# Retention attention fused with a two-layer MLP: attention work of two tiles grouped on TensorE, and PSUM laid out as named double banks

## Chip, cores, metric

One core of one Trainium2 chip. The metric is device time in microseconds of one execution; most executions of one kernel agree within 0.3%. In the profile PE is TensorE (matmuls), PEld its weight loads, DVE VectorE, ACT ScalarE, POOL GpSimd and SP the engine that issues most DMAs. The span is the time from the first to the last instruction of the profiled run.

## The reference

```python
# q, k, v: (8, 8, 576, 64); w_in: (512, 2048); w_out: (2048, 512); all f32
scores = (q @ k.transpose(0, 1, 3, 2)) / 8
gamma  = 1 - 2.0 ** (-5 - arange(8))                  # one per head
D      = where(i >= j, gamma ** (i - j), 0)           # causal decay
x      = ((scores * D) @ v).transpose(0, 2, 1, 3).reshape(4608, 512)
h      = x @ w_in
out    = (h * cos(h)) @ w_out
```

## The kernel before

The tokens are cut into 36 tiles of 128. For each tile: `prep` scales q and k by powers of gamma, `transposes` turns them, `scores` makes the products within the tile (64-row matmuls, two heads at a time in the array), which DVE then masks into `ret`, `state` carries the sum over earlier tiles of a sequence, `attn_out` adds both parts (full matmuls for the state, then matmuls of 64 columns for the tile itself) and casts the result to `xT`. Blocks of 512 tokens (two of 256 near the start) then go through `mm1` (h, cosine, product) and `mm2` (o). The attention of the next block is put between the o matmuls of the present one. Both kernels divide PSUM, where matmul results go, into eight banks of 512 f32 columns; an h tile is what one cosine and one product then read.

```python
widths = [512, 256, 256] + [512] * 7
ps_sc = tc.tile_pool(name="ps_sc", bufs=1, space=PSUM)    # scores: 2 banks
ps_st = tc.tile_pool(name="ps_st", bufs=1, space=PSUM)    # state: 1
ps_ov = tc.tile_pool(name="ps_ov", bufs=1, space=PSUM)    # attention output: 1
ps_mm = tc.tile_pool(name="ps_mm", bufs=4, space=PSUM)    # h, o, transposes: 4
# ... cut
def attn_out(g):
    ps = ps_ov.tile([P, HG, P], F32, tag="ov")
    if c > 0:                              # 4 matmuls 128x128 with the state
        # ... cut
    for hg in range(HG):                   # 8 matmuls of 64 columns
        for he in range(2):
            nc.tensor.matmul(ps[he*D : he*D+D, hg, :], lhsT=vb[:, 2*hg+he, :],
                             rhs=ret[:, he, hg, :], ...)
    nc.vector.tensor_copy(xT[:, :, g*P : (g+1)*P], ps)

def units(g0, g1):                         # order of the attention pieces
    # transposes (early tiles), scores(g), attn_out(g - 1), state(g), ...
    # ... cut
def mm1(n, et, c0, w):
    ps = ps_mm.tile([P, 512 // w, w], F32, tag="mm", name="h")
    # matmuls into one bank, then
    nc.scalar.activation(cosh, ps, ACTF.Sin, bias=half_pi, scale=1.0)
    nc.vector.tensor_mul(gT[:, et : et + m, c0 : c0 + w], ps, cosh)
# ... cut: in each block the units are spread evenly between the 64 mm2 calls
```

## Time and profile before

| | before |
|---|---|
| median of 16 runs | 326.04 us (325.43 to 327.14) |
| span of the profiled run | 324.5 us |
| PE / DVE / ACT / POOL busy | 94% / 59% / 41% / 30% |
| first h matmul of block 1, 2, 3, 4 and 9 (PE timeline) | 58.48, 76.06, 96.24, 129.30, 293.19 us |
| one middle block of 512 tokens | 32.51 or 33.06 us |

Blocks are counted from 0; 1 and 2 are the small ones. The stretch up to the first h matmul of block 1 is set by arriving data, the rest by PE. Blocks 4 to 7 have these two lengths in turn because the work repeats every nine tiles (two sequences of 576 tokens), and the first and the last of the nine skip four state matmuls each: a block that holds both has 217 matmuls, the others 225. Line numbers (L272 and so on) are those of each kernel by itself. The lines that the argument rests on are in the prediction.

### The profile page before, as it was taken

Reading aid. Unit: us, or ns where it says so; the run is one execution under the profiler, and the core shown is the slowest. Engines: PE = TensorE matmul, PEld = TensorE weight load, DVE = VectorE, ACT = ScalarE, POOL = GpSimd, SP = SyncE. Lnnn points to the kernel's source line nnn. Section 1 sums busy time; section 2 is a strip of 40 time slices with the busy share of each in tenths; the row PEclk is TensorE's granted clock in tenths of the full one; section 3 lists DMA queues with packets and bytes.
Section 4 is the critical chain, followed back from the end, with each engine's and each line's share of the span. In section 5 each row is a group of like instructions: output and inputs, shape, how many; then the busy total and the mean of one; then the engine's idle time right before and its main releaser. Section 6 shows DMA issues by size and latency. Waiting matters only on the chain.

```text
span 324.5 us, 5550 instructions
## 1 busy us (share of the span) xinstructions
PE 306.6 (94%) x2176; PEld 160.9 (50%) x2176; DVE 192.1 (59%) x267; ACT 133.8 (41%) x204; POOL 97.8 (30%) x120
## 2 busy tenths in 40 slices
PE   2687999999899999999999999999999999999995
PEld 1565844857554445444444454444445444454442
DVE  2765705565877854685468646864686558645800
ACT  4344722544218511751176107610761067016711
POOL 3370057644463635430543054305430000000000
PEclk9999999999999999999999999999999999999999
DMA  9999999999999999935993599449942500010011
GB/s 171 216 124 209 210 205 244 225 211 217 187 237 199 258 214 254 225 68 134 207 253 58 134 237 211 67 113 252 215 71 65 129 35 3 32 68 32 0 67 65
DMA packets 151514, 49.65 MB, mean 153 GB/s; under 512 B 142784, under 2 KB 146368, under 8 KB 151488
## 3 DMA queue, kind: packets, MB, share of 16 engines
q1 hardware_dynamic: 147264, 45.10, 72.7%
q0 software_dynamic: 4224, 4.19, 8.1%
q8 instruction: 17, 0.28, 0.4%
q14 instruction: 9, 0.07, 0.1%
HBM read 36.70 MB, written 9.44 MB: 142 GB/s over the span
## 4 chain that ended last, share of the span: by engine, by line
PE 83%; DMA 8%; SPq 5%; POOL 2%; issue 1%; ACT 0%; DVE 0%; DVEq 0%
PE o L272 38%; PE h L256 34%; DMA w_out_sb<-in_moe_w_out_dram 5%; SPq L102 5%; PE ov L219 3%; PE sc L155 3%; DMA fq<-in_q_dram 3%; PE st L183 2%; PE ov L209 2%; POOL w_in_sb L334 1%; POOL qks L125 1%; PE tr L142 0%; DVE ret L164 0%; POOL qks L126 0%; ACT cosh L264 0%
## 5 line engine op out<-in xcount | busy, mean ns | idle before, releaser
L272 PE MATMUL o<-w_out_sb,gT 128*128 128x512 bf16 x576 | 142.5, 380 | 0.4 <-DMA w_out_sb<-in_moe_w_out_dram 0.4
L256 PE MATMUL h<-xT,w_in_sb 128*128 128x512 bf16 (+1 forms) x704 | 127.7, 342 | 2.3 <-DMA w_in_sb<-in_moe_w_in_dram 2.3
L265 DVE TENSOR_TENSOR gT<-h,cosh 128x512 bf16<-128x512 f32 x144 | 99.5, 691 | 47.8 <-ACT cosh L264 47.8
L264 ACT ACTIVATE cosh<-h,half_pi 128x512 f32<-128x512 f32 x144 | 98.9, 687 | 31.3 <-PE h L256 31.3
L256 PEld LDWEIGHTS <-w_in_sb 128*128 128x128 bf16 x704 | 69.0, 98 | 59.5 <-DMA w_in_sb<-in_moe_w_in_dram 2.8
L281 ACT COPY ot<-o 128x512 f32<-128x512 f32 x36 | 21.1, 585 | 143.6 <-PE o L272 143.6
L125 POOL TENSOR_TENSOR qks<-fq,gq 128x512 bf16<-128x512 f32 x36 | 37.5, 1042 | 127.8 <-DMA fq<-in_q_dram 116.1
L272 PEld LDWEIGHTS <-gT 128*128 128x128 bf16 x576 | 49.6, 98 | 52.0 <-issue 0.7
L164 DVE TENSOR_TENSOR ret<-sc,tri 128x1024 bf16<-128x1024 f32 x32 | 39.1, 1222 | 20.6 <-PE sc L155 20.5
L227 DVE CAST xT<-ov 128x512 bf16<-128x512 f32 x36 | 24.8, 689 | 19.1 <-PE ov L219 19.0
L126 POOL TENSOR_TENSOR qks<-fk,gk 128x512 bf16<-128x512 f32 x32 | 33.3, 1042 | 3.9 <-DMA fk<-in_k_dram 2.5
L192 DVE TENSOR_TENSOR sb<-st,diag 128x512 bf16<-128x512 f32 x32 | 22.0, 688 | 13.2 <-PE st L183 13.1
L132 POOL CAST vb<-fv 128x512 bf16<-128x512 f32 x32 | 19.5, 610 | 9.0 <-DMA fv<-in_v_dram 7.3
L155 PE MATMUL sc<-qkT 64*128 64x128 bf16 x288 | 15.2, 228 | 4.2 <-ACT qkT L147 2.9
L155 PEld LDWEIGHTS <-qkT 64*128 64x128 bf16 x288 | 8.7, 98 | 18.8 <-issue 13.2
L219 PE MATMUL ov<-ret,vb 128*64 128x128 bf16 x288 | 15.8, 234 | 1.6 <-DVE ret L164 1.6
L147 ACT COPY qkT<-tr 128x512 bf16<-128x512 bf16 x16 | 8.8, 589 | 12.0 <-PE tr L142 12.0
L183 PEld LDWEIGHTS <-qks 128*128 128x128 bf16 (+1 forms) x128 | 9.6, 101 | 8.1 <-issue 2.5
L209 PEld LDWEIGHTS <-sb 128*128 128x128 bf16 x128 | 10.1, 102 | 7.0
L183 PE MATMUL st<-vb,qks 128*128 128x128 bf16 (+1 forms) x128 | 13.3, 230 | 0.0
L219 PEld LDWEIGHTS <-vb 128*64 128x64 bf16 x288 | 10.0, 114 | 6.2 <-issue 3.4
L209 PE MATMUL ov<-qkT,sb 128*128 128x128 bf16 (+1 forms) x128 | 12.7, 224 | 0.0
(29 smaller groups left out, 35.2 us busy)
## 6 DMA issues: line engine op xcount, KB each, us to landing
out_dram<-ot SPq DMA_DIRECT2D x36, 256.0 KB, 3.7
fq<-in_q_dram SPq DMA_DIRECT2D x32, 256.0 KB, 4.2
fk<-in_k_dram SPq DMA_DIRECT2D x32, 256.0 KB, 4.6
fv<-in_v_dram SPq DMA_DIRECT2D x32, 256.0 KB, 4.9
w_out_sb<-in_moe_w_out_dram POOLq DMA_DIRECT2D x4, 512.0 KB, 17.9
w_in_sb<-in_moe_w_in_dram POOLq DMA_DIRECT2D x1, 1024.0 KB, 12.7
fq<-in_q_dram SPq DMA_DIRECT2D x8, 128.0 KB, 4.0
fk<-in_k_dram SPq DMA_DIRECT2D x8, 128.0 KB, 4.1
```

Source lines behind the costliest of these rows:

```text
L125: nc.gpsimd.tensor_tensor(out=qks[:, 0], in0=fq, in1=tq, op=ALU.mult)
L126: (nc.vector if early else nc.gpsimd).tensor_tensor(out=qks[:, 1], in0=fk, in1=tk, op=ALU.mult)
L155: nc.tensor.matmul(ps[:, he, hg, :], lhsT=qkT[d0 : d0 + D, HG + hg, :], rhs=qkT[d0 : d0 + D, hg, :], start=True, stop=True,)
L164: nc.vector.tensor_tensor(out=ret.rearrange("p a b i -> p (a b) i"), in0=ps.rearrange("p a b i -> p (a b) i"), in1=mask.unsqueeze(1).to_br ...
L183: nc.tensor.matmul(ps[:, hg, :], lhsT=qks[p0:, 1, 2 * hg : 2 * hg + 2, :].rearrange("s h d -> s (h d)"), rhs=vb[p0:, 2 * hg : 2 * hg + 2, ...
L209: nc.tensor.matmul(ps[:, hg, :n], lhsT=sb[:, hg, :], rhs=qkT[:, hg, :n], start=(hg == 0), stop=False, skip_group_check=True,)
L219: nc.tensor.matmul(ps[he * D : he * D + D, hg, :], lhsT=vb[:, 2 * hg + he, :], rhs=ret[:, he, hg, :], start=(c == 0 and hg == 0), stop=(hg ...
L227: nc.vector.tensor_copy(xT[:, :, g * P : (g + 1) * P], ps)
L256: nc.tensor.matmul(ps[:, j, :], lhsT=w_in_sb[:, dg, (et + j) * P : (et + j + 1) * P], rhs=xT[:, dg, t0 : t0 + w], start=(dg == 0), stop=(d ...
L264: nc.scalar.activation(cosh, ps, ACTF.Sin, bias=half_pi, scale=1.0)
L265: nc.vector.tensor_mul(gT[:, et : et + m, c0 : c0 + w], ps, cosh)
L272: nc.tensor.matmul(ps, lhsT=gT[:, et, tsi * P : (tsi + 1) * P], rhs=w_out_sb[:, et, :], start=(et == 0), stop=(et == ET - 1),)
```

## The change

Its intent: let the attention pieces of two neighbouring tiles run together, and let ACT and DVE work on 1024 columns at a time. For that the PSUM pools become named buffers in one pool: a, b and m of two banks each, n and st of one. Besides, w_in is loaded in four equal pieces, two small products move from DVE to POOL, and block 3 runs in half widths so that it can start before its second half is ready. Not shown in the cut below: x is kept in one rotating tile for each block, some SBUF pools have a buffer more, the o tiles that share a double bank are called `oo`, and the places of the attention pieces are now fixed numbers.

```diff
-    ps_sc/ps_st/ps_ov (bufs=1), ps_mm (bufs=4)
+    psum = ctx.enter_context(tc.tile_pool(name="psum", bufs=1, space=bass.MemoryType.PSUM))
@@ prep
-        (nc.vector if early else nc.gpsimd).tensor_tensor(
+        (nc.vector if early and g in (0, 3) else nc.gpsimd).tensor_tensor(
@@ attn_out, now for a list of tiles
+        ps = psum.tile([P, len(gs), HG, P], F32, tag=bank, name="ov")
+        for x, g in enumerate(gs):      # all full matmuls with the state first
...
+        for x, g in enumerate(gs):      # then all matmuls of 64 columns
...
+        nc.vector.tensor_copy(tiles["x", n][...], ps)      # one cast for the pair
@@ mm1
-        m = 512 // w
+        m = 1024 // w
-        ps = ps_mm.tile([P, m, w], F32, tag="mm", name="h")
+        ps = psum.tile([P, m, w], F32, tag=bank, name="h")
@@ loads
-            load_w_in(0, 256); load_w_in(256, 512); load_w_in(512, 1024); load_w_in(1024, 2048)
+            for e in range(0, DF, 512):
+                load_w_in(e, e + 512)
@@ placement between the o matmuls
+    def pair(g, banks, sc, av):
+        mid = (sc + av) // 2
+        return [
+            (sc - 5, lambda: state(g)),
+            (sc, lambda: (scores(g, banks[0]), scores(g + 1, banks[1]))),
+            (mid, lambda: state(g + 1)),
+            (av, lambda: attn_out([g, g + 1], banks[0])),
+        ]
...
+        banks = {0: "bambambam", 1: "bmab", 2: "bmab", 3: "mamabmab"}.get(n, "bmabmabm")
...
+        elif n == 2:
+            todo = pair(g, "ab", 11, 24) + pair(g + 2, "ba", 31, 40)[:2]
+            late += [lambda: (state(g + 3), attn_out([g + 2, g + 3], "b"))]   # inside block 3
+        elif n + 1 < len(widths):
+            todo = pair(g, "ab", 12, 26) + pair(g + 2, "ab", 41, 56)
```

More of the change, by code (lines that the diff above doesn't have):

```diff
@@ L60 @@
     trp = ctx.enter_context(tc.tile_pool(name="trp", bufs=8))
-    retp = ctx.enter_context(tc.tile_pool(name="retp", bufs=3))
-    stp = ctx.enter_context(tc.tile_pool(name="stp", bufs=3))
+    retp = ctx.enter_context(tc.tile_pool(name="retp", bufs=4))
+    stp = ctx.enter_context(tc.tile_pool(name="stp", bufs=4))
     gp = ctx.enter_context(tc.tile_pool(name="gp", bufs=2))
@@ L65 @@
     op = ctx.enter_context(tc.tile_pool(name="op", bufs=4))
-    ps_sc = ctx.enter_context(tc.tile_pool(name="ps_sc", bufs=1, space=bass.MemoryType.PSUM))
-    ps_st = ctx.enter_context(tc.tile_pool(name="ps_st", bufs=1, space=bass.MemoryType.PSUM))
-    ps_ov = ctx.enter_context(tc.tile_pool(name="ps_ov", bufs=1, space=bass.MemoryType.PSUM))
-    ps_mm = ctx.enter_context(tc.tile_pool(name="ps_mm", bufs=4, space=bass.MemoryType.PSUM))
+    xp = ctx.enter_context(tc.tile_pool(name="xp", bufs=3))
+    psum = ctx.enter_context(tc.tile_pool(name="psum", bufs=1, space=bass.MemoryType.PSUM))
     ctx.enter_context(tc.manual_schedule())
@@ L86 @@
     w_out_sb = consts.tile([P, ET, DM], BF16)
-    xT = consts.tile([P, DG, NTOK], BF16)
     tiles = {}
@@ L132, in prep, with transposes @@
             nc.gpsimd.tensor_copy(vb, tiles.pop(("fv", g)))
-    def transposes(g):
+    def transposes(g, early=False):
         qks, vb, qkT = tiles["a", g]
@@ L139, in transposes @@
         for m in range(2):
-            ps = ps_mm.tile([P, HG, P], BF16, tag="mm", name="tr")
+            ps = psum.tile([P, 2 * HG, P], BF16, tag=("bn" if early else "ba" if g < 6 else "ma")[m], name="tr")
             for hg in range(HG):
@@ L146, in transposes, with scores @@
                 )
-            nc.scalar.copy(qkT[:, m * HG : (m + 1) * HG, :], ps)
-    def scores(g):
+            nc.scalar.copy(qkT[:, m * HG : (m + 1) * HG, :], ps[:, :HG, :])
+    def scores(g, bank):
         qks, vb, qkT = tiles["a", g]
-        ps = ps_sc.tile([P, 2, HG, P], F32, tag="sc", name="sc")
+        ps = psum.tile([P, 2, HG, P], F32, tag=bank, name="sc")
         for hg in range(HG):
@@ L178, in state @@
         if first:
-            tiles["stps"] = ps_st.tile([P, HG, P], F32, tag="st", name="st")
+            tiles["stps"] = psum.tile([P, HG, P], F32, tag="st", name="st")
         ps = tiles["stps"]
@@ L198, in state, with attn_out @@
         tiles["sb", g + 1] = sb
-    def attn_out(g):
-        c = g % PER
-        qks, vb, qkT = tiles.pop(("a", g))
-        ret = tiles.pop(("ret", g))
-        ps = ps_ov.tile([P, HG, P], F32, tag="ov", name="ov")
-        if c > 0:
+    def attn_out(gs, bank):
+        ps = psum.tile([P, len(gs), HG, P], F32, tag=bank, name="ov")
+        for x, g in enumerate(gs):
+            c = g % PER
+            if c == 0:
+                continue
+            qkT = tiles["a", g][2]
             sb = tiles.pop(("sb", g))
@@ L209, in attn_out @@
                 nc.tensor.matmul(
-                    ps[:, hg, :n],
+                    ps[:, x, hg, :n],
                     lhsT=sb[:, hg, :],
@@ L216, in attn_out @@
                 )
-        for hg in range(HG):
-            for he in range(2):
-                nc.tensor.matmul(
-                    ps[he * D : he * D + D, hg, :],
-                    lhsT=vb[:, 2 * hg + he, :],
-                    rhs=ret[:, he, hg, :],
-                    start=(c == 0 and hg == 0),
-                    stop=(hg == HG - 1),
-                    skip_group_check=True,
-                )
-        nc.vector.tensor_copy(xT[:, :, g * P : (g + 1) * P], ps)
-    def units(g0, g1):
-        u = []
-        if g0 < min(g1, N_PE_T):
-            u.append(lambda g=g0: transposes(g))
-        for g in range(g0, g1):
-            if g + 1 < min(g1, N_PE_T):
-                u.append(lambda g=g + 1: transposes(g))
-            u.append(lambda g=g: scores(g))
-            if g > g0:
-                u.append(lambda g=g - 1: attn_out(g))
-            if g % PER < PER - 1:
-                u.append(lambda g=g: state(g))
-        if g1 > g0:
-            u.append(lambda g=g1 - 1: attn_out(g))
-        return u
@@ L246, in mm1 @@
-    def mm1(n, et, c0, w):
+        for x, g in enumerate(gs):
+            vb = tiles.pop(("a", g))[1]
+            ret = tiles.pop(("ret", g))
+            for hg in range(HG):
+                for he in range(2):
+                    nc.tensor.matmul(
+                        ps[he * D : he * D + D, x, hg, :],
+                        lhsT=vb[:, 2 * hg + he, :],
+                        rhs=ret[:, he, hg, :],
+                        start=(g % PER == 0 and hg == 0),
+                        stop=(hg == HG - 1),
+                        skip_group_check=True,
+                    )
@@ L248, in mm1 @@
+        n = max(m for m in range(len(starts)) if starts[m] <= gs[0] * P)
+        if ("x", n) not in tiles:
+            tiles["x", n] = xp.tile([P, DG, 512], BF16, tag="xT", name="xT")
+        t0 = gs[0] * P - starts[n]
+        nc.vector.tensor_copy(
+            tiles["x", n][:, :, t0 : t0 + len(gs) * P].rearrange("p c (x i) -> p x c i", i=P), ps
+        )
+    def mm1(n, et, c0, w, bank):
         if ("g", n) not in tiles:
             tiles["g", n] = gp.tile([P, ET, 512], BF16, tag="gT", name="gT")
-        gT = tiles["g", n]
@@ L251, in mm1 @@
-        m = 512 // w
-        t0 = starts[n] + c0
-        ps = ps_mm.tile([P, m, w], F32, tag="mm", name="h")
+        gT, xT = tiles["g", n], tiles["x", n]
+        m = 1024 // w
+        ps = psum.tile([P, m, w], F32, tag=bank, name="h")
         for j in range(m):
@@ L258, in mm1 @@
                     lhsT=w_in_sb[:, dg, (et + j) * P : (et + j + 1) * P],
-                    rhs=xT[:, dg, t0 : t0 + w],
+                    rhs=xT[:, dg, c0 : c0 + w],
                     start=(dg == 0),
@@ L268, in mm2 @@
         gT = tiles["g", n]
+        wide = tsi == 0 if n == 2 else tsi in (1, 3)
         if et == 0:
-            tiles["o", n, tsi] = ps_mm.tile([P, DM], F32, tag="mm", name="o")
-        ps = tiles["o", n, tsi]
+            if not wide:
+                tiles["o"] = psum.tile([P, DM], F32, tag="n", name="o")
+            elif tsi < 2:
+                tiles["oo"] = psum.tile([P, 2, DM], F32, tag="m", name="oo")
+        ps = tiles["oo"][:, tsi // 2, :] if wide else tiles["o"]
         nc.tensor.matmul(
@@ L347 @@
         if g == 3:
-            load_w_in(0, 256)
-            load_w_in(256, 512)
-            load_w_in(512, 1024)
-            load_w_in(1024, 2048)
+            for e in range(0, DF, 512):
+                load_w_in(e, e + 512)
             w_dma = [load_w_out(e, e + 4) for e in range(0, ET, 4)]
@@ L356 @@
             nc.gpsimd.memset(tri_mix[:HP, HP:], 0.0)
-        transposes(g)
+        transposes(g, early=True)
         nc.scalar.copy(tiles["a", g][1], tiles.pop(("fv", g)))
-        scores(g)
+        scores(g, "a")
         if g < 3:
@@ L363 @@
         if g < 3:
-            attn_out(g)
+            attn_out([g], "m")
     for g in (4, 5):
@@ L367 @@
     loaded = prepared = transposed = 6
-    first = [(0, 0), (0, 4), (1, 0), (0, 8), (1, 4), (0, 12), (1, 8), (1, 12)]
-    for i, (half, et) in enumerate(first):
-        mm1(0, et, half * 256, 256)
-        if i == 0:
-            attn_out(3)
-        mm1(0, et + 2, half * 256, 256)
-    for n, w in enumerate(widths):
-        if n > 0:
-            for et in range(0, ET, 512 // w):
-                mm1(n, et, 0, w)
-        todo = []
-        if n + 1 < len(widths):
-            g0 = starts[n + 1] // P
-            todo = units(g0, g0 + widths[n + 1] // P)
-        nts = w // P
-        mms = [(tsi, et) for tsi in range(nts) for et in range(ET)]
-        lo, hi = (len(mms) // 2, len(mms) - 4) if n == 0 else (2, len(mms) - 6)
-        place = [lo + (hi - lo) * i // max(1, len(todo) - 1) for i in range(len(todo))]
+    def pair(g, banks, sc, av):
[6 more added lines that the diff above has]
+        ]
@@ new lines, in pe_transposes @@
+    def pe_transposes(g, place):
+        return [(place, lambda: transposes(g)), (place + 6, lambda: transposes(g + 1))]
+    late = []
+    for n, w in enumerate(widths):
+        if n in (0, 3):
+            halves = [(0, 0), (0, 4), (1, 0), (0, 8), (1, 4), (0, 12), (1, 8), (1, 12)]
+            if n == 3:
+                halves.sort()
+            blocks = [(et, half * 256, 256) for half, et in halves]
+        else:
+            blocks = [(et, 0, w) for et in range(0, ET, 1024 // w)]
+        banks = {0: "bambambam", 1: "bmab", 2: "bmab", 3: "mamabmab"}.get(n, "bmabmabm")
+        for i, (et, c0, cw) in enumerate(blocks):
+            mm1(n, et, c0, cw, banks[i])
+            if n == 0 and i == 0:
+                attn_out([3], "m")
+            if n == 3 and i == 1:
+                late.pop()()
+        g = starts[n] // P + w // P
+        if n == 0:
+            todo = [(28, lambda: transposes(g)), (40, lambda: transposes(g + 1))]
+            todo += pair(g, "ab", 46, 58)
+        elif n == 1:
+            todo = pe_transposes(g, 1) + pair(g, "ab", 13, 26)
+        elif n == 2:
[3 more added lines that the diff above has]
+            todo = pair(g, "ab", 12, 26) + pair(g + 2, "ab", 41, 56)
+        else:
+            todo = []
+        todo.sort(key=lambda u: u[0])
+        mms = [(tsi, et) for tsi in range(w // P) for et in range(ET)]
@@ L389 @@
         for i, (tsi, et) in enumerate(mms):
-            while place and place[0] <= i:
-                place.pop(0)
-                todo.pop(0)()
+            while todo and todo[0][0] <= i:
+                todo.pop(0)[1]()
             mm2(n, tsi, et)
+        assert not todo
 _INS = ['q', 'k', 'v', 'moe_w_in', 'moe_w_out']
```

## The prediction

> **What bounds the kernel now.** I read the page first, then the chain that ended last, then the TensorE timeline around single insertions. The page, and the chain by engine:
>
> ```profile
> span 324.5 us, 5550 instructions
> PE 306.6 (94%) x2176; PEld 160.9 (50%) x2176; DVE 192.1 (59%) x267; ACT 133.8 (41%) x204; POOL 97.8 (30%) x120
> ...
> DMA  9999999999999999935993599449942500010011
> ...
> PE 83%; DMA 8%; SPq 5%; POOL 2%; issue 1%; ACT 0%; DVE 0%; DVEq 0%
> ```
>
> PE is the bound: it makes 83% of the chain, and the rest (DMA, SP's queue, POOL) lies in the first 50 us, where operands are still arriving. DVE at 59% and ACT at 41% have room. But 94% busy does not mean 94% of what PE can do, so I looked at steady blocks of 512 tokens (64 matmuls of h, 64 of o, and the attention of four 128-token tiles put between the o matmuls). Windows from block start to block start; the columns are length, then busy time of PE, PEld, DVE, ACT, POOL, then clock, DMA share and GB/s:
>
> ```profile
> 129.47:161.98 32.51, 32.51 (x217) 15.36 (x216) 20.61 (x27) 13.33 (x20) 10.55 (x13) 1.00 0.84 161
> 161.98:195.04 33.06, 33.06 (x225) 15.77 (x224) 21.29 (x28) 13.33 (x20) 11.33 (x13) 1.00 0.88 169
> ```
>
> PE never idles here, so only the start-to-start distance of its matmuls can shrink. In the chain the 64 h matmuls of a block take 13.81 us, 0.216 each. Around a scores insertion (8 matmuls with 64 rows), a state insertion (4 matmuls of 128x128) and an output insertion (4 full matmuls, then 8 with 64 columns), the PE timeline reads (start, length, what):
>
> ```profile
> 143.33 0.38 PE L272 MATMUL o<-w_out_sb,gT 128*128 128x512 bf16 x1
> 143.64 0.40 PE L155 MATMUL sc<-qkT 64*128 64x128 bf16 x8
> 143.97 0.39 PE L272 MATMUL o<-w_out_sb,gT 128*128 128x512 bf16 x1
> ```
>
> ```profile
> 145.06 0.39 PE L183 MATMUL st<-vb,qks 128*128 128x128 bf16 x4
> 145.28 0.38 PE L272 MATMUL o<-w_out_sb,gT 128*128 128x512 bf16 x1
> ```
>
> ```profile
> 148.09 0.39 PE L209 MATMUL ov<-qkT,sb 128*128 128x128 bf16 x4
> 148.41 0.41 PE L219 MATMUL ov<-ret,vb 128*64 128x128 bf16 x8
> 148.76 0.39 PE L272 MATMUL o<-w_out_sb,gT 128*128 128x512 bf16 x1
> ```
>
> State: 145.06 to 145.28 is 0.22 for four, 0.055 each, nothing lost. Scores: o starts at 143.33 and the scores at 143.64, 0.31 where 0.216 is normal, so 0.095 lost on entry; scores to o is 0.33 where eight matmuls running in twos need 4 x 0.055 = 0.22, so 0.11 lost on exit. Output: 148.09 to 148.41 is 0.32 for four full matmuls that need 0.22 (0.10 lost), and 148.41 to 148.76 is 0.35 for 0.22 (0.12 lost, rounded up). **Every visit to a 64-row or 64-column shape costs 0.21 to 0.22 us**, and a block of four tiles makes eight such visits: 1.7 us in 33.
>
> What PE waits for, other than that (engine, line, whom; us in total, times, longest), from the waits of PE:
>
> ```profile
> PE h L256 <- DMA w_in_sb<-in_moe_w_in_dram: 2.3, 2, 1.3
> PE ov L219 <- DVE ret L164: 1.6, 3, 0.9
> PE sc L155 <- DVE ret L164: 1.3, 1, 1.3
> ...
> PE o L272 <- DMA w_out_sb<-in_moe_w_out_dram: 0.4, 1, 0.4
> PE tr L142 <- POOL qks L126: 0.4, 1, 0.4
> ```
>
> Only the third lies after 60 us (at 85.8 us): the single scores buffer is still being read.
>
> **What the Trainium skill says.** "TensorEngine Tiling (Array Packing)", Key Properties: changing the tiling mode drains the TensorE, changing only the tile does not. The trace agrees: 0.095 to 0.12 us at each change between full and 64-wide shapes, none between o and st. "TensorE: Matmul & The Clock Gate", Back-to-back issue gap, gives N/2.4 + 2.5 ns: 216 ns at 512 columns and 56 at 128; the trace has 0.216 and 0.055. "Trainium Kernel Development and Optimization", Performance Expectations, warns that matmul busy time is a poor metric since matmuls are pipelined; here one o matmul is listed at 380 ns while the next starts after 216. "PSUM — Partial Sum Buffer", PSUM bank collisions, asks for guarding by bank: a bank that DVE or ACT is reading is closed to PE. That decides whether fewer, wider buffers can rotate; the 1.3 us wait above is such a case.
>
> **The change part by part.**
> 1. *Pairing.* Scores of two tiles run back to back, then later the outputs of two tiles (all full matmuls first, then all sixteen of 64 columns). Four visits per pair become two: 2 x 0.215 = 0.43 us saved. Tiles 4 to 35 are paired, 16 pairs: 16 x 0.43 = **6.9 us**, all on PE's path. Tiles 0 to 3 stay single.
> 2. *The wait at 85.8 us* goes, since two scores buffers exist: **-1.3**. In its place the block of tokens 1024 to 1535 starts with its second h tile in the bank of a scores read just issued: about 1.7 us of h matmuls against two reads of 1.22 us each (the `ret` row of the page's groups) plus a start-up: my estimate **+0.3**.
> 3. *h in two banks* (1024 columns): 72 cosines and 72 products instead of 144 each. DVE takes 0.691 us for 512 columns and 1.22 for 1024 (`ret`), so 99.5 us of products become about 72 x 1.22 = 88; ACT saves some too. Neither is on the path: **0**. What can hurt is the latency: after PE ends a 1.73 us tile, cosine (at most 1.22) and product (1.22) hold its banks for 2.5 us, but with three double banks PE returns after 2 x 1.73 = 3.46. The first o matmul that needs the last product is the 15th, 14 x 0.216 = 3.0 us later. Both hold with 0.5 to 1 us to spare.
> 4. *Block 3 in half widths*: 128 x 0.109 (6.99 us for 64 in the chain) against 64 x 0.216: **+0.15**.
> 5. *Start.* Before 43 us DMA sets the pace. The first two w_in transfers, 256 columns each, become one of 512, and packets double. While they ran, the DMA view gives the first line below, later the second:
>
> ```profile
> DMA packets 1107, 0.59 MB, mean 132 GB/s; under 512 B 32, under 2 KB 1106, under 8 KB 1106
> ...
> DMA packets 1703, 2.07 MB, mean 207 GB/s; under 512 B 48, under 2 KB 1332, under 8 KB 1703
> ```
>
> 0.59 MB at 207 would take 2.9 us instead of 4.5; I credit about half, 0.8. PE's own waits on w_in (2.3 us) vanish or shrink, but they are worth nothing by themselves: the o matmuls then start earlier and wait for the last w_out piece, which landed at 43.04 and only moves by what the DMA stream gains. After that, later transposes (index 28 and 40 instead of 32 and 35) avoid the 0.4 us wait for POOL. Together **-1.2**. The products for k of tiles 1 and 2 move from DVE (0.68) to POOL (1.04), which otherwise idles for q: hidden, **0**.
> 6. *Casts of 1024 columns* (0.69 becomes about 1.22) six o matmuls (1.3 us) ahead of the next block in the two small blocks, and transposes there into a bank just used: **+0.2**.
>
> Sum: -6.9 - 1.3 + 0.3 + 0.15 - 1.2 + 0.2 = -8.75, so 325.9 becomes 317.1; I say 317.0. The tail (last o, copy, store) stays.
>
> **Rivals.** (a) *PSUM becomes the new wait.* Eight banks are now shared by named buffers used one at a time, and one late reader stops PE in every block. For: the margins in 3 are under 1 us and DVE runs its queue in order. Against: DVE is 59% busy and will be less. A stall of 0.5 us in each of seven blocks would give 320.5; 1 us would give 324. (b) *The drain is not saved by adjacency*: the loss belongs to each scores group and not to the change of shape, or two groups in different banks drain too. For: the view before shows no two groups of one shape in a row. Against: inside a group, eight matmuls take 0.22 plus exactly one exit. Then only items 2, 4, 5 and 6 remain, -1.85: 324.0. (c) *The start gains nothing*, as DMA is full from 18 to 150 us and q/k/v behind it come no sooner: 318.3. (d) *The start gains more*, with the whole w_in and w_out stream over a microsecond sooner: 316.
>
> **Range and chances.** The pairing term is counted from the trace and I trust it within 1 us; the stalls can only add, up to about 3 us, and the start can give 1 us more. So 314.5 to 320.5. The 2% line is at 319.4: faster 0.80, same 0.19, slower 0.01.
>
> **What would show each step.** Blocks from the fourth on should be 0.85 us shorter (32.2 and 31.65 instead of 33.06 and 32.51). Scores should come as 16 in about 0.66 us from entry to exit, with one entry loss of 0.095 and one exit of 0.11. The waits of PE should show no more than a few tenths on cosines, products, `ret` or casts; if they show over 2 us there, rival (a) holds and I am too low. If paired groups are as long as two single ones, (b) holds. The last w_out wait should end near 42.2 us rather than 43.04. The PE total of busy time should fall to about 298 us, and the h products on DVE should be 72 of about 1.22 us.

## The result

The changed kernel takes **317.31 us** (median of 8 runs, 316.98 to 317.88) against 326.04. The ratio is 0.9733, with a 95% interval of 0.9722 to 0.9743. The forecast was 317.0.

The page after: PE still makes 82% of the chain, and is busy for a slightly larger share of a shorter span.

```profile
span 315.4 us, 5447 instructions
PE 299.8 (95%) x2240; PEld 168.0 (53%) x2240; DVE 175.1 (56%) x177; ACT 115.0 (36%) x132; POOL 99.5 (32%) x122
...
PE 82%; DMA 8%; SPq 4%; POOL 2%; DVE 1%; issue 1%; ACT 1%
```

The two kinds of middle block after, windows of the same columns as in the prediction; 31.63 against 32.51, and 32.18 against 33.06, **0.88 us less each**:

```profile
124.69:156.32 31.63, 31.63 (x217) 15.57 (x216) 18.84 (x17) 11.25 (x12) 12.99 (x15) 1.00 1.04 202
156.32:188.50 32.18, 32.18 (x225) 15.83 (x224) 19.43 (x18) 11.25 (x12) 10.13 (x13) 1.00 0.85 161
```

Why, in the PE timeline after. The scores of two tiles come as sixteen:

```profile
140.94 0.38 PE L269 MATMUL o<-w_out_sb,gT 128*128 128x512 bf16 x1
141.25 0.62 PE L154 MATMUL sc<-qkT 64*128 64x128 bf16 x16
141.80 0.39 PE L269 MATMUL o<-w_out_sb,gT 128*128 128x512 bf16 x1
```

The entry is still 0.31 and one exit remains: 0.55 from scores to o, against 8 x 0.055 = 0.44 for sixteen matmuls running in twos. Two separate groups took 2 x (0.31 - 0.216 + 0.33) = 0.85; the pair takes 0.31 - 0.216 + 0.55 = 0.64. The outputs of two tiles:

```profile
144.83 0.61 PE L211 MATMUL ov<-qkT,sb 128*128 128x128 bf16 x8
145.37 0.64 PE L224 MATMUL ov<-ret,vb 128*64 128x128 bf16 x16
145.94 0.39 PE L269 MATMUL oo<-w_out_sb,gT 128*128 128x512 bf16 x1
```

The pair takes 1.11 us from its first matmul to the next o matmul, against 2 x (148.76 - 148.09) = 1.34.

PE's waits after, without those of the first 25 us that both kernels share; the wait of scores on `ret` is gone, and no new one in the middle is longer than 0.3:

```profile
PE h L249 <- DVE xT L236: 0.6, 1, 0.6
PE tr L141 <- POOL qks L125: 0.5, 1, 0.5
PE tr L141 <- DVE gT L258: 0.3, 1, 0.3
PE o L269 <- DMA w_out_sb<-in_moe_w_out_dram: 0.3, 1, 0.3
...
PE h L249 <- DVE ret L163: 0.2, 1, 0.2
```

The products of h, first before, then after (groups of instructions: busy time, mean ns of one, idle before):

```profile
L265 DVE TENSOR_TENSOR gT<-h,cosh 128x512 bf16<-128x512 f32 x144 | 99.5, 691 | 47.8 <-ACT cosh L264 47.8
```

```profile
L258 DVE TENSOR_TENSOR gT<-h,cosh 128x1024 bf16<-128x1024 f32 x72 | 88.1, 1224 | 63.7 <-ACT cosh L257 63.5
```

DVE does 11 us less of them and waits 16 us longer: what it saves becomes waiting.

Where the 9.1 us of the spans come from, by the first h matmul of each block in the PE timelines:

| stretch | before | after | saved | forecast |
|---|---|---|---|---|
| start to block 1 | 58.48 | 56.44 | 2.04 | 0.43 (one pair) + 1.2 |
| block 1 | 17.58 | 17.53 | 0.05 | 0.43, less most of 0.2 |
| blocks 2 and 3 | 53.24 | 50.55 | 2.69 | 4 x 0.43 + 1.3 - 0.3 - 0.15 = 2.57 |
| blocks 4 to 8 | 163.89 | 159.49 | 4.40 | 10 x 0.43 = 4.3 |
| block 9 and tail | 31.3 | 31.4 | 0 | 0 |

The start, lines of the PE timeline before and after (the waits are in brackets):

```profile
43.04 4.48 PE L272 MATMUL o<-w_out_sb,gT 128*128 128x512 bf16 x20 [0.43 <-DMA w_out_sb<-in_moe_w_out_dram]
...
49.43 0.40 PE L142 MATMUL tr<-ident,qks 128*128 128x128 bf16 x4 [0.38 <-POOL qks L126]
```

```profile
41.24 1.02 PE L269 MATMUL o<-w_out_sb,gT 128*128 128x512 bf16 x4 [0.26 <-DMA w_out_sb<-in_moe_w_out_dram]
...
48.62 0.40 PE L141 MATMUL tr<-ident,qks 128*128 128x128 bf16 x4 [0.51 <-POOL qks L125]
```

The last w_out piece lets PE go on 1.8 us earlier, but the transposes of tile 5 then wait for POOL at least as long as before (0.51 against 0.38).

### The profile page after: what moved, and what is told of

It reads as the page before. It is cut to its first block, busy times and chain, and to the rows that moved or that the text cites. A ratio compares the mean times of both kernels' runs of the same rounds, so it can differ in the third digit from the quotient of the medians.

```text
span 315.4 us, 5447 instructions
## 1 busy us (share of the span) xinstructions
PE 299.8 (95%) x2240; PEld 168.0 (53%) x2240; DVE 175.1 (56%) x177; ACT 115.0 (36%) x132; POOL 99.5 (32%) x122
## 4 chain that ended last, share of the span: by engine, by line
PE 82%; DMA 8%; SPq 4%; POOL 2%; DVE 1%; issue 1%; ACT 1%
PE h L249 34%; PE oo L269 19%; PE o L269 19%; DMA w_out_sb<-in_moe_w_out_dram 5%; SPq L101 4%; DMA fq<-in_q_dram 3%; PE ov L224 3%; PE sc L154 3%; PE st L182 2%; PE ov L211 2%; POOL w_in_sb L331 1%; POOL qks L124 1%; DVE ret L163 0%; DVE gT L258 0%; PE tr L141 0%
## 5 line engine op out<-in xcount | busy, mean ns | idle before, releaser
L249 PE MATMUL h<-xT,w_in_sb 128*128 128x256 bf16 (+1 forms) x768 | 128.2, 328 | 1.0 <-DVE xT L236 0.6
L258 DVE TENSOR_TENSOR gT<-h,cosh 128x1024 bf16<-128x1024 f32 x72 | 88.1, 1224 | 63.7 <-ACT cosh L257 63.5
L249 PEld LDWEIGHTS <-w_in_sb 128*128 128x128 bf16 x768 | 75.4, 98 | 52.6 <-issue 1.5
L257 ACT ACTIVATE cosh<-h,half_pi 128x1024 f32<-128x1024 f32 x72 | 80.1, 1113 | 54.7 <-PE h L249 54.7
L269 PE MATMUL o<-w_out_sb,gT 128*128 128x512 bf16 x288 | 71.0, 380 | 0.3 <-DMA w_out_sb<-in_moe_w_out_dram 0.3
L269 PE MATMUL oo<-w_out_sb,gT 128*128 128x512 bf16 x288 | 69.0, 380 | 0.0
L236 DVE CAST xT<-ov 128x1024 bf16<-128x1024 f32 (+1 forms) x20 | 22.3, 1116 | 25.2 <-PE ov L224 25.0
L278 ACT COPY ot<-oo 128x512 f32<-128x512 f32 x18 | 10.5, 585 | 66.8 <-PE oo L269 66.8
L278 ACT COPY ot<-o 128x512 f32<-128x512 f32 x18 | 10.5, 585 | 58.9 <-PE o L269 58.9
L141 PE MATMUL tr<-ident,qks 128*128 128x128 bf16 x64 | 7.1, 265 | 6.3 <-POOL qks L124 5.3
```

What stands on the lines that cost most here:

```text
L236: nc.vector.tensor_copy(tiles["x", n][:, :, t0 : t0 + len(gs) * P].rearrange("p c (x i) -> p x c i", i=P), ps)
L249: nc.tensor.matmul(ps[:, j, :], lhsT=w_in_sb[:, dg, (et + j) * P : (et + j + 1) * P], rhs=xT[:, dg, c0 : c0 + w], start=(dg == 0), stop=(d ...
L269: nc.tensor.matmul(ps, lhsT=gT[:, et, tsi * P : (tsi + 1) * P], rhs=w_out_sb[:, et, :], start=(et == 0), stop=(et == ET - 1),)
```

## The experiments

**Theory.** PE loses about 0.21 us at every visit to a shape of 64 rows or 64 columns, and the change halves the visits of tiles 4 to 35. **Rival.** The gain is from the wide tiles and the new banks, or the loss belongs to each group whatever stands next to it. A second rival was that PSUM waits would eat the gain.

### Control

> Control: the changed kernel itself, unedited, on the chip of the next three runs. Every theory expects 317.3 us, 0.973 of the kernel before.

317.45 us (5 runs), ratio 0.9734, 0.9721 to 0.9748. The result repeats.

### Taking the pairs apart

```diff
# e1_sc_apart
-            (sc, lambda: (scores(g, banks[0]), scores(g + 1, banks[1]))),
+            (sc - 3 * (sc == 31), lambda: scores(g, banks[0])),
+            (sc + 3 * (sc != 31), lambda: scores(g + 1, banks[1])),
# e2_ov_apart
-            (av, lambda: attn_out([g, g + 1], banks[0])),
+            (av - 3, lambda: attn_out([g, g + 1], banks[0], 0)),   # first tile
+            (av, lambda: attn_out([g, g + 1], banks[0], 1)),       # second tile, then the one cast
# e3_both_apart: both
```

> The two scores groups of each pair are taken apart by three o matmuls; banks, casts and everything else stay. Main theory (each visit to a 64-row shape costs PE a fixed loss on entry and exit): 16 more visits of 0.21 us, so +3.4 us, 320.7. Rival (the gain is from the wide h tiles and the new banks, the loss belongs to each group and not to the change of shape): no change, 317.3.

> The outputs of the two tiles of a pair run apart, three o matmuls (once an h tile) between; one cast for both stays. Main theory: 16 more visits to the 64-column shape of 0.22 us, +3.5 us, 320.8. Rival (gain from wide tiles and banks): 317.3.

> Scores and outputs both apart: the pairing undone, all else of the change kept. Main theory: +6.9 us, 324.2, that is only some 1.8 us faster than the kernel before. Rival: 317.3.

| | us | ratio to before | middle blocks | per pair |
|---|---|---|---|---|
| control | 317.45 | 0.9734 | 31.63, 32.18 | |
| scores apart | 320.30 | 0.9824 | 32.05, 32.61 | 0.21 |
| outputs apart | 322.36 | 0.9883 | 32.08, 32.64 | 0.23 |
| both apart | 325.52 | 0.9981 | 32.52, 33.06 | 0.44 |

The block lengths are the clean measure (there are two pairs in a block). Windows of `e3_both_apart`:

```profile
127.92:160.44 32.52, 32.52 (x218) 15.39 (x217) 18.86 (x17) 11.27 (x12) 12.56 (x15) 1.00 0.87 173
160.44:193.50 33.06, 33.06 (x226) 15.77 (x225) 19.46 (x18) 11.26 (x12) 10.51 (x12) 1.00 0.90 155
```

With the pairing undone and the wide tiles, new banks and single casts kept (17 and 18 DVE instructions in a block against 27 and 28 before), the blocks have the length they have in the kernel before, within 0.01 us. So in these blocks the pairing is the whole gain, and with the pairs apart the wide tiles bring nothing. The rival falls.

Over the control, e2 takes 4.9 us more and e3 8.1, that is 1.4 and 1.2 us above the expected 3.5 and 6.9. For e2 that is an artefact of my edit: it put the second half of the late output in block 3 one h tile later, and the cast then held up PE:

```profile
PE h L253 <- DVE xT L240: 1.4, 2, 1.2
```

The profile of e3 has the same 1.2 us wait. e1 takes 2.85 us more than the control, 0.5 less than expected. Its middle blocks say 0.42 and 0.43; but its block 1 starts 0.2 us before the control's (56.42 against 56.65) where one more visit should make it 0.2 later, and blocks 2 and 3 grow by 0.5 where four visits are worth 0.8, with the 0.2 us wait of h on `ret` gone.

### Dose

```diff
-            (sc, lambda: (scores(g, banks[0]), scores(g + 1, banks[1]))),
+            (sc, first half of scores(g)), (sc + 1, second half),
+            (sc + 2, first half of scores(g + 1)), (sc + 3, second half),
```

> Dose: the sixteen scores matmuls of each pair in four visits of four, one o matmul between, instead of one visit. Main theory, linear in the visits: 3 x 16 x 0.21 = 10.1 us more than the changed kernel, 327.5, and each middle block 1.27 us longer (32.9 and 33.45 instead of 31.63 and 32.18). Rival (the loss is per group of a tile, or taken by waits for the reads of scores): not linear, 320 to 324, or waits on the mask products appear.

327.24 us (4 runs, ratio 1.0036). Windows:

```profile
128.16:161.07 32.91, 32.91 (x217) 15.56 (x216) 18.84 (x17) 11.25 (x12) 12.77 (x15) 1.00 0.89 170
161.07:194.52 33.45, 33.45 (x225) 15.78 (x224) 19.45 (x18) 11.24 (x12) 9.93 (x12) 1.00 0.79 151
```

One visit per pair gives 31.63, two give 32.05, four give 32.91: 0.42 for two more visits in the block, 0.86 for the four after that. The loss is 0.21 us a visit and linear, and PE is never idle in these windows: it shows as busy.

The weight loads of the kernel before show what is different at such a change. First those of the scores group and of the o matmul after it, then those of the state group (full shape) of the prediction:

```profile
143.64 0.23 PEld L155 LDWEIGHTS <-qkT 64*128 64x128 bf16 x8 [0.42 <-issue]
143.97 0.11 PEld L272 LDWEIGHTS <-gT 128*128 128x128 bf16 x2
```

```profile
144.85 0.43 PEld L183 LDWEIGHTS <-qks 128*128 128x128 bf16 x4
```

The state group's first load starts 0.21 us before its first matmul (145.06), while the matmul in front still runs. At a change of shape the load starts only with its own matmul (143.64 and 143.97). So in these groups weights are loaded ahead within a shape and not across a change. Whether the lost 0.1 us is that load or the emptying of the array, no run separates.

### Are the wide tiles worth anything by themselves?

```diff
# e4_narrow: after each bank of the double bank
+            if (j + 1) % k == 0:
+                nc.scalar.activation(cosh, ps[:, j0 : j + 1, :], ...)
+                nc.vector.tensor_mul(gT[...], ps[:, j0 : j + 1, :], cosh)
# e4b_narrow: after both banks
+        for j0 in (0, k):
+            nc.scalar.activation(cosh, ps[:, j0 : j0 + k, :], ...)
+            nc.vector.tensor_mul(gT[...], ps[:, j0 : j0 + k, :], cosh)
```

> Cosine and product of h by single banks of 512 columns again (144 of each), in the same double banks; pairing kept. Main theory (DVE and ACT are off the path, the wide tiles bring nothing by themselves): 317.4, within 0.4 us of the changed kernel, though DVE is busy about 11 us more. Rival (fewer and wider instructions are part of the gain): 2 us or more slower, 319.5 or above.

> The narrow cosines and products again, now issued only after all matmuls of a double bank, so that PE never writes a bank tile of which a half is being read (in e4 PE waited 1.6 us for a product in each tile). Main theory: 317.4 within 0.4 us of the changed kernel, with DVE and ACT busy about 11 and 19 us longer. Rival (fewer and wider instructions are part of the gain): 319.5 or above.

Both misses: 440.26 and 332.16 us (ratios 1.3506 and 1.0188). Neither measures what I meant to measure. In e4 PE waits for the first product of a double bank before it writes the second bank, and in e4b the second cosine waits for the first product, each 72 times. PE's waits in e4, then all waits in e4b:

```profile
PE h L249 <- DVE gT L261: 112.4, 72, 1.6
```

```profile
ACT cosh L259 <- DVE gT L260: 56.4, 72, 1.4
```

In e4b cosine, product, cosine, product of one double bank run one after the other, and a double bank comes out every 2.05 us (products start at 140.62 and 142.66), while PE needs 1.73. The halves lie in different banks, so the Trainium skill's rule ("PSUM — Partial Sum Buffer", PSUM bank collisions: guard by bank) would allow the overlap. The waits are those of the program, which orders the engines by buffer; that it is by buffer is my reading of the waits, which no run isolates. So the question as asked stays open. `e3_both_apart` answers it in another way, for unpaired attention: narrow tiles in single banks (the kernel before) and wide tiles in double banks give the same block length. No run pairs the attention with narrow tiles in single banks. What e4 and e4b add: **within a double bank the wide form is needed**.

### How much room the bank rotation has

```diff
-.get(n, "bmabmabm")
+.get(n, "babababa")
```

> The h tiles of the last six blocks rotate through two double banks instead of three; all else kept. My estimate of the margin: a bank is held 1.73 us by PE, 1.11 by the cosine, 1.22 by the product and 0.25 between them, 4.3 in all, so two banks give a tile each 2.15 us instead of 1.73. Some 7 tiles x 0.42 = 2.9 us in each of six blocks, 17.6 in all: 335, with waits of h on products. If PE does not notice, the margin with three banks is larger than I thought.

333.65 us (one look). In its windows the block that took 31.63 takes 34.32, and PE is idle for 2.2 of it, waiting for products (13.2 us in 18 waits over the whole run; the other 0.5 us of the block shows as busy):

```profile
124.50:158.82 34.32, 32.12 (x217) 15.52 (x216) 18.84 (x17) 11.24 (x12) 13.09 (x15) 1.00 0.96 187
```

Predicted 2.9 us a block, measured 2.7. Two banks are too few by 0.4 us a tile; three are enough, as the absence of waits in the changed kernel shows. That is why the second rival did not come about.

### The late outputs of block 3

```diff
-        if n in (0, 3):                 # half widths
+        if n == 0:
-            if n == 3 and i == 1:
-                late.pop()()
...
+        while late:                     # at the end of block 2 instead
+            late.pop()()
```

> Block 3 in full width, the outputs of tiles 10 and 11 before it instead of inside it. Saves the 0.15 us of the half widths and the 0.2 us wait, but PE now waits for both mask products and for the cast with nothing to do: about 1.3 + 1.4 us. Net +2.4, 319.8. If the wait of the kernel before at this spot was harmless, no change.

320.01 us (4 runs, ratio 0.9816), 2.6 us more than the control. PE waits for the cast and for the mask product:

```profile
PE h L249 <- DVE xT L236: 1.3, 1, 1.3
PE h L249 <- DVE gT L258: 0.7, 1, 0.7
PE ov L211 <- DVE ret L163: 0.6, 1, 0.6
```

So the half widths, whose cost the prediction put at 0.15 us, together with the late outputs that they make room for, pay for themselves well.

### The start

```diff
# e5_old_w_in: the four loads as before (256, 256, 512, 1024 columns)
# e6_k_dve
-        (nc.vector if early and g in (0, 3) else nc.gpsimd).tensor_tensor(
+        (nc.vector if early else nc.gpsimd).tensor_tensor(
```

> w_in loaded as before in pieces of 256, 256, 512 and 1024 columns. My term of the prediction: the last w_out piece lands 0.8 us later and the kernel ends 0.8 us later, 318.2. The first h tile needs the first 512 columns and both small pieces, the fourth needs the last 1024; if these waits overrun the slack before the w_out wait, it is more, up to 319. If the start gains nothing from the pieces: 317.4.

> The products for k of tiles 1 and 2 back on DVE. Expected by every theory: no change, 317.4 within 0.3, since w_in lands later than PE needs it.

e5: 317.77 us (5 runs), ratio 0.9753 (0.9737 to 0.9770) against 0.9734 for the control: 0.0019 x 326 = 0.6 us, with intervals that overlap. Its profile, of the slowest of the five runs (318.72), has the sign expected: the last w_out transfer lands 21.1 us after its issue, against 21.7 before and 19.9 in the changed kernel, and PE waits 1.0 us for w_in, where the changed kernel waits 0.2. In the window from 17.5 to 22 us the DMA view of the changed kernel and then of e5 read:

```profile
DMA packets 713, 0.73 MB, mean 162 GB/s; under 512 B 16, under 2 KB 712, under 8 KB 712
```

```profile
DMA packets 1103, 0.62 MB, mean 138 GB/s; under 512 B 29, under 2 KB 1102, under 8 KB 1102
```

Two thirds of the packets bring more bytes. e6: 316.82 us (4 runs), ratio 0.9722 (0.9707 to 0.9737), so 0.4 us faster than the control if anything; with two chips and overlapping intervals I call that no difference shown. The start before block 1 varied by 0.6 us between profiles of kernels that are the same there (first h matmul of block 1 at 56.08 to 56.65 us in the changed kernel, the control, e7 and e10), so neither is resolved better.

### A version meant to be better

```diff
-            (sc - 5, lambda: state(g)),
+            (sc - 5 * (g % PER != MIX), lambda: state(g)),
-            (mid, lambda: state(g + 1)),
+            (sc if (g + 1) % PER == MIX else mid, lambda: state(g + 1)),
# transposes of tiles 6 and 7: all eight into one bank of m, one copy
```

> A version meant to beat both. First, the state matmuls of the four middle tiles (64 rows) are put next to the scores, which have 64 rows too, so that their own visit goes: 4 x 0.21 = 0.84 us. Second, the transposes of tiles 6 and 7 go into one bank with one copy each, in place of a second bank that was still being read: 0.3 us. Main theory: 316.3. If the loss belongs to each group and not to the change of shape: 317.1, only the second part.

**316.28 us** (4 runs, ratio 0.9706, 0.9691 to 0.9721): 0.9 us less than the control by the ratios, the fastest kernel here. Windows:

```profile
123.95:155.58 31.63, 31.31 (x214) 15.56 (x216) 18.85 (x17) 11.27 (x12) 12.83 (x15) 1.00 1.04 205
155.58:187.55 31.97, 31.65 (x222) 15.89 (x224) 19.35 (x18) 11.27 (x12) 10.70 (x13) 1.00 0.82 161
```

The block with a middle tile, whose state matmuls have 64 rows, falls from 32.18 to 31.97; the block without one stays at 31.63. (The idle 0.3 us in each is where a few matmul records are missing: counts are 214 and 222 instead of 217 and 225.) Blocks 3 and 7 fall by 0.20 and 0.21. In block 7 the PE timeline reads:

```profile
244.24 0.62 PE L164 MATMUL sc<-qkT 64*128 64x128 bf16 x16
244.70 0.38 PE L192 MATMUL st<-vb,qks 64*128 64x128 bf16 x4
245.02 1.69 PE L279 MATMUL o<-w_out_sb,gT 128*128 128x512 bf16 x7
```

Sixteen scores take 0.46 us to the state matmuls, where they take 0.55 to an o matmul: no exit is paid between the two. So the loss is one of changing shape: a 64-row group of another kind next to the scores does not pay it. (For tile 22, in block 5, the state matmuls come first and alternate with scores in the trace; the block gains no more than the others, so that overlap brings nothing.) The second edit brought 0.13 instead of 0.3 us in block 1 (17.40 instead of 17.53).

## Why the prediction was right

1. *The pairing, 16 x 0.43 = 6.9.* Right in mechanism and size: 0.44 per pair (the outputs' exit was read as 0.12 where 0.35 - 0.22 is 0.13; e2 has 0.23 a visit), by undoing it (e1, e2, e3), by dose (e9) and by extending it to another 64-row group (v2). In the changed kernel itself blocks 4 to 8 fall by 0.88 each, and 0.85 was foretold.
2. *The wait at 85.8 us goes, a smaller one comes.* Right: the 1.3 us wait is gone, and the new one on `ret` is 0.2 us where I had 0.3.
3. *Wide tiles bring nothing.* Right for unpaired attention, shown by e3's block lengths; the paired blocks save 0.88 each, and the pairing explains all of it. My step from there in e4 and e4b, that narrow tiles in the same double banks would do as well, was wrong, though the forecast of the time did not use it.
4. *Half widths +0.15.* Blocks 2 and 3 together saved 2.69 where the terms sum to 2.57; this term was not isolated. What it buys is 2.6 us (e7).
5. *The start, -1.2.* About right in sum (2.04 less the 0.43 of its pair is 1.6) but not in its parts. "I credit about half, 0.8" for the DMA stream was too low: PE goes on at 41.24, not 42.2. "Later transposes avoid the 0.4 us wait for POOL" was wrong: PE arrived earlier too, and q and k of tile 5 did not come as much earlier, so 0.5 us was waited there. That the pieces of w_in make the stream faster has the right sign in e5 (0.6 us), but that run alone would not prove it.
6. *Casts and transposes, +0.2.* Block 1 saved 0.05 where its pair is worth 0.43, so 0.38 was lost there: 0.3 on a product that still held the bank of a transpose, the rest unexplained. The term was too small by about 0.2 us.

That the forecast is within 0.3 us is partly luck. The start saved 0.4 us more than forecast and block 1 0.2 less, which cancel in part, and 0.3 is less than the 0.6 by which the start alone varied between profiles. The two profiled runs differ by 9.1 us of span, the medians by 8.73 us, because the profiled run of the kernel before (326.48 us) is one of its slower ones.

PE's busy time fell to 299.8 us and not to about 298. The 298 fits only if the waits are taken off the busy time too, which they are not part of: the terms that are busy time give 306.6 - 6.9 + 0.15 = 299.9.

Rival (a), PSUM waits, did not come, and e10 shows how near it was: one double bank less and it costs 2.7 us a block. Rival (b) fell with e1 to e3 and e9. Of (c) and (d), the start came out between, nearer to (d).

## What to carry to other kernels

When an engine is "never idle" and still the bound, look at the start-to-start distance of its instructions around every change of kind: on TensorE a full-array stream that is interrupted by a group of 64 rows or 64 columns pays about 0.21 us each time, which the profile books as busy. Collect such groups, as many as PSUM can hold, and put other groups of the same shape next to them. Count how long a PSUM buffer is held (write, first reader, second reader) against the time until its turn comes again before handing out fewer, wider buffers.

## What the Trainium skill lacked or had wrong

- "TensorEngine Tiling (Array Packing)", Key Properties, says that a change of tiling mode drains the TensorE, but gives no cost. Here: 0.095 us on entry to 64 rows and 0.11 on exit, 0.21 to 0.23 a visit, linear from one to four visits a pair (31.63, 32.05, 32.91 us a block); and the next weight load then starts only with its own matmul.
- "TensorE: Matmul & The Clock Gate", Back-to-back issue gap, gives 131 ns a matmul at 512 columns and 81 ns at 128 as the sustained rate of real streams with weight loads, and calls N/2.4 + 2.5 the isolated gap. Here the formula holds in the stream: 64 matmuls of 512 columns, each with its weight load, take 13.81 us, 216 ns each, and four of 128 columns take 0.22 us, 55 each.
- "DMA: Bandwidth & Descriptors", Specifications, names 512 B as the least transfer for line rate. Rows of 256 bf16 columns are 512 B; in the window from 17.5 to 22 us, where such pieces ran, the stream moved 132 to 138 GB/s, and with rows of 1 KB (the changed kernel) 162. The last of these windows starts with some 0.9 us of little traffic, the others with at most 0.2; other causes were not separated.
- No page that I read works out how many buffers such a chain of matmul, cosine and product needs. Here (1.73, 1.11 and 1.22 us for 1024 columns) two double banks make a block of eight tiles 2.7 us longer, and three do not stall it.
